# Block-sorted attention with a gated MLP behind it: q turned by DMA, other layouts on both sides of PSUM, a new written order and a guarded second path

## The chip, the cores and the metric

The program runs on one core of a Trainium2 chip. The metric is device time of one launch in microseconds (us). TensorE (PE in the profile) multiplies and puts its results into PSUM; ScalarE (ACT) and VectorE (DVE) bring them from there into SBUF; GpSimd (POOL) works on SBUF alone and issues the loads; SyncE (SP) issues the other DMAs.

## The reference

Inputs: q, k and v as 4 batches x 8 heads x 768 positions x 64 numbers, float32; `sort_net`, an 8x8 matrix for each batch and head; and the weights of a gated MLP.

```
P = sort_net
for _ in range(5):
    P = exp(P - max(P, -1));  P /= sum(P, -1) + 1e-9;  P /= sum(P, -2) + 1e-9
k_sorted[i] = sum_j P[i, j] * k_block[j]          # 8 blocks of 96 positions; v alike
attn  = softmax(q_block[i] @ k_sorted[i].T / 8) @ v_sorted[i]
x     = attn, heads side by side                    # 4 x 768 x 512
h     = relu(x @ w_in);  u, v = h[:, :512], h[:, 512:]
v_n   = (v - mean) / sqrt(var + 1e-6)               # over the 512 columns
gated = u * (w_spatial @ v_n + b_spatial)           # w_spatial is 768 x 768
out   = gated @ w_out
```

The kernel multiplies in bfloat16 and adds up in float32.

## The kernel before

Nothing is scheduled by a library. A string, `ORDER` (L16), lists units of work, and each unit issues its instructions on each engine's queue in that order. An engine takes its queue in order, so a unit that waits holds all that is listed later on the same engine. Heads go in pairs (`hp`, 0 to 3), and the 8 blocks of a sequence in halves (`ih`, 0 and 1). PSUM is four tiles of two banks, `ps0` to `ps3`; a unit's first number names the one that it fills, and its letter the engine that empties it (A is ACT, D is DVE).

The units in the order in which a batch passes them, with their lines:

- `L` (L153): loads, issued by POOL; float32 in HBM, bfloat16 in SBUF. Partition p holds positions 6p to 6p+5 of every head, so one block of 96 positions is 16 partitions. `wv` and `wu` are the halves of w_in, `ws` is w_spatial, `wo` is w_out.
- `SK` (L190): one of five rounds on P, one exp on ACT and six small DVE instructions. The last writes `p_x`, half of it on DVE and half on POOL. `PR`/`PS` (L209, L213) turn it on PE, `P0` (L223) spreads it into `pd`, a 128x128 mixing matrix for each head of batch 0, and `PD` (L236) does so on POOL for the other batches.
- `QT` (L270): turns q of a head pair with 12 matmuls against the identity; the result is emptied into `qT`.
- `KT` (L298): mixes and turns k with 12 matmuls against `pd`; emptied into `kT`. Both copies read PSUM straight on and write every sixth element, so that positions come into their natural order (first snippet below).
- `VM` (L309) and `VC` (L323): mix v into `vm`, and bring it from 16 partitions x 6 positions to 96 partitions with eight DMAs on SP for each batch.
- `SC` (L333): scores of half the blocks of a head pair, 8 matmuls, and one exp on ACT into `ex`. `AT` (L355): 8 matmuls with v (a column of ones gives the sum), and on DVE a reciprocal and a multiplication into `x_sb`.
- `XT` (L378): turns x with 8 PE transposes; emptied into `xT`.
- `VP` (L398), `LN`, `LA` (L423, L429): the v half of x @ w_in, relu, statistics on DVE, normalisation. `UP` (L438): the u half. `WS` (L251): turns w_spatial on PE, six units in all. `SP` (L453): 12 matmuls with w_spatial, the bias added into `z`, and the product with u, on DVE or POOL, into `gt`. `OP` (L473): 8 matmuls with w_out, emptied, and stored by SP.

```
copy(eng, q_tile(b, hp)[:, lo * G:(lo + n) * G].rearrange("p (x g) -> p g x", g=G),   # L282
     t[:, 0:n * G].rearrange("p (g x) -> p g x", g=G))
```

Of the kernel before, what the change touches and what calls it, by code (L numbers as in the profile page):

```python
# [9 lines left out]
BF16 = mybir.dt.bfloat16  # L10
AF = mybir.ActivationFunctionType
# [3 lines left out]

ORDER = """  # L16
L:q:0:0:64 ID IN L:v:0:0:128 SK:0 L:k:0:0:128 SK:0 QT:0:A:0:2:0 L:q:0:64:128 L:wv SK:0 QT:1:A:0:3:0
QT:2:A:0:0:0 QT:3:A:0:1:0 SK:0 DM:0:5:384 DM:1:5:384 DM:2:5:384 DM:3:5:384 L:wu IV:0 L:ws SK:1 PR:0
PS P0:0:0:2 P0:0:2:8 P0:1:4:8 P0:1:0:4 PC:D KT:1:A:0:2:0 L:v:1:0:128 VM:2:D:0:3 VM:3:A:0:0 VM:1:D:0:2
VM:0:A:0:1 KT:2:A:0:0:0 QT:3:D:0:1:1 KT:1:D:0:1:0 KT:0:D:0:3:0 IV:1 KT:2:D:0:2:1 SC:3:0:2:0  # L20
L:k:1:0:128 VC:0:0 KT:1:A:0:0:1 VC:0:1 SC:0:0:0:0 KT:2:D:0:1:1 QT:3:D:0:2:1 KT:1:D:0:3:1 L:q:1:0:128
SC:2:0:3:0 QT:0:D:0:3:1 SC:3:0:1:0 AT:1:0:2:0 PD:1:0:4 QT:2:A:0:0:1 AT:0:0:0:0 SC:3:0:3:1 SC:1:0:1:1
AT:2:0:3:0 AT:0:0:1:0 SC:3:0:2:1 XT:1:D:0:0:1 L:wo SC:2:0:0:1 XT:3:D:0:0:0 AT:0:0:1:1 PD:1:4:8
AT:1:0:3:1 WS:2:A:1 L:v:2:0:128 VP:3:D:0:0:1 L:k:2:0:128 WS:0:A:3 VP:2:A:0:2 VM:1:A:1:2 VM:3:A:1:0
UP:0:A:0:0:0 VM:2:A:1:1 AT:1:0:2:1 UP:3:A:0:1:0 AT:0:0:0:1 KT:1:A:1:2:2 XT:2:D:0:1:1 VM:3:A:1:3
WS:0:D:2 KT:1:A:1:0:2 KT:2:D:1:1:2 KT:3:A:1:3:2 VC:1:0 PD:3:4:8 VC:1:1 WS:0:D:4 WS:1:D:0 QT:2:A:1:2:2
QT:3:D:1:3:2 QT:0:A:1:1:2 QT:1:D:1:0:2 SC:2:1:2:0 XT:3:D:0:1:0 SC:0:1:3:1 SC:1:1:2:1 AT:2:1:2:0
PD:2:0:4 VP:3:A:0:5 SC:0:1:0:1 AT:1:1:3:1 L:q:2:0:128 LN:0:0:3 WS:2:A:5 LA:0:2 VP:3:D:0:3:4
SC:0:1:3:0 SC:1:1:0:0 UP:2:A:0:0:1 AT:0:1:2:1 VM:3:A:2:1 PD:2:4:8 UP:1:A:0:1:1 AT:2:1:0:1 L:v:3:0:128
AT:3:1:0:0 SC:0:1:1:1 KT:1:A:2:2:2 XT:2:D:1:1:1 VM:0:A:2:0 AT:3:1:1:1 SC:1:1:1:0 VM:2:D:2:2  # L30
L:k:3:0:128 KT:0:A:2:3:2 XT:3:D:1:1:0 QT:1:A:2:0:2 VM:2:A:2:3 LA:0:1 AT:0:1:1:0 LN:0:3:6 VC:2:0
UP:3:A:1:0:1 LA:0:0 LA:0:4 XT:1:D:1:0:0 KT:2:A:2:0:2 LA:0:3 VC:2:1 LA:0:5 QT:0:A:2:2:2 AT:3:1:3:0
VP:1:A:1:4:5 SC:2:2:0:1 PD:3:0:4 SC:0:2:0:0 LN:1:4:6 SP:3:P:0:1 SC:1:2:2:1 SC:2:2:2:0 SP:0:P:0:2
XT:3:D:1:0:1 AT:1:2:0:0 L:q:3:0:128 SP:2:D:0:3 LA:1:4 KT:0:A:2:1:2 QT:3:A:2:1:2 QT:1:A:2:3:2
AT:2:2:0:1 SP:0:P:0:0 VM:3:A:3:1 AT:1:2:2:0 VP:2:D:1:0:1 SC:0:2:3:0 SC:3:2:1:1 VP:1:A:1:2:3
VM:0:D:3:3 UP:2:A:1:1:0 LN:1:0:4 OP:3:A:0:2 AT:1:2:2:1 LA:1:2 LA:1:0 LA:1:5 LA:1:1 UP:2:A:1:0:0
LA:1:3 SC:0:2:3:1 SC:3:2:1:0 OP:1:A:0:0 AT:2:2:3:1 OP:0:A:0:1 AT:3:2:1:1 AT:1:2:1:0 UP:2:A:1:1:1
XT:0:D:2:1:1 XT:3:D:2:1:0 KT:1:A:3:3:2 QT:2:A:3:1:2 KT:0:A:3:1:2 KT:3:D:3:0:2 VP:1:D:2:4:5 VM:2:A:3:2
VM:3:A:3:0 SP:0:D:1:3 XT:1:A:2:0:0 AT:2:2:3:0 SP:3:P:1:2 LN:2:4:6 LA:2:4 UP:1:A:2:0:1 XT:0:D:2:0:1
QT:2:A:3:2:2 VC:3:0 LA:2:5 KT:3:A:3:2:2 QT:1:D:3:3:2 QT:0:D:3:0:2 VP:2:D:2:2:3 VC:3:1 UP:3:A:2:0:0  # L40
SP:1:D:1:1 SC:0:3:2:0 SC:2:3:1:1 SP:3:D:1:0 SC:1:3:2:1 SC:0:3:3:1 UP:2:A:2:1:0 AT:3:3:1:1
UP:1:A:2:1:1 AT:0:3:2:0 VP:2:D:2:0:1 SC:3:3:1:0 SC:1:3:0:0 OP:0:A:1:2 AT:2:3:3:1 LN:2:0:4 AT:3:3:2:1
OP:1:A:1:0 SC:0:3:3:0 SC:2:3:0:1 OP:3:A:1:1 LA:2:0 LA:2:1 LA:2:3 LA:2:2 AT:1:3:0:0 SP:0:D:2:1
SP:2:P:2:2 XT:1:A:3:1:1 AT:3:3:0:1 SP:0:D:2:0 AT:2:3:3:0 XT:1:A:3:1:0 SP:3:P:2:3 AT:0:3:1:0
UP:1:A:3:0:1 UP:2:A:3:1:1 XT:3:A:3:0:0 XT:0:D:3:0:1 VP:1:A:3:4:5 VP:2:A:3:2:3 VP:0:A:3:0:1 OP:3:A:2:0
UP:1:A:3:0:0 LN:3:4:6 LA:3:4 LN:3:0:4 LA:3:0 LA:3:5 LA:3:3 OP:2:A:2:2 LA:3:2 UP:0:A:3:1:0 LA:3:1
OP:3:D:2:1 SP:1:P:3:1 SP:2:D:3:3 SP:0:D:3:0 SP:3:D:3:2 OP:1:A:3:2 OP:2:A:3:1 OP:0:A:3:0
"""

# [10 lines left out]
def kernel(  # L60
# [92 lines left out]
    def u_L(what, *a):  # L153
        if what in ("q", "k", "v"):
            load(what, int(a[0]), int(a[1]), int(a[2]), int(a[1]) == 0)
        elif what == "wv":
            nc.gpsimd.dma_start(
                out=w_in_sb[:, :, DH:DFF], in_=moe_w_in.rearrange("(kc p) f -> p kc f", p=128)[:, :, DH:DFF])
        elif what == "wu":
            nc.gpsimd.dma_start(  # L160
                out=w_in_sb[:, :, 0:DH], in_=moe_w_in.rearrange("(kc p) f -> p kc f", p=128)[:, :, 0:DH])
        elif what == "ws":
            nc.gpsimd.dma_start(out=wsp_nat, in_=moe_w_spatial.rearrange("(c p) s -> p c s", p=128))
        elif what == "wo":
            nc.gpsimd.dma_start(out=w_out_sb, in_=moe_w_out.rearrange("(fc p) n -> p fc n", p=128))

    def u_IN():
        nc.sync.dma_start(out=p_all, in_=sort_net.rearrange("b h i j -> (b h) i j"))
        nc.sync.dma_start(
            out=b_bc, in_=_raw_ap(moe_b_spatial, 0, [[0, 128], [1, S]]))  # L170
        nc.vector.memset(warm, 0.0)
        nc.vector.memset(eps_tile, 1e-6)
        for n in range(NE):
            nc.vector.memset(ex[n][:, 2 * NI * BLK:], 0.0)

    def u_ID():
        make_identity(nc, ident)
        nc.vector.reduce_sum(
            out=st["m32"][:], in_=ident.rearrange("p (j t) -> p t j", t=TB), axis=AX.X)
        nc.vector.tensor_copy(out=mask16, in_=st["m32"][:])  # L180

    st["m32"] = const.tile([128, TB], FP32, name="m32")

    def u_IV(n):
        n = int(n)
        nc.gpsimd.memset(vm[n][:, :, :, D:VW], 1.0)
        nc.gpsimd.memset(vb[n][:, :, :, D:VW], 1.0)


    def u_SK(last):  # L190
        nc.scalar.activation(out=p_all, in_=p_all, func=AF.Exp)
        nc.vector.reduce_sum(out=rowsum, in_=p_all, axis=AX.X)
        nc.vector.reciprocal(out=rowsum, in_=rowsum)
        nc.vector.tensor_mul(out=p_all, in0=p_all, in1=rowsum.to_broadcast([BH, NB, NB]))
        nc.vector.reduce_sum(out=colsum, in_=p_all.rearrange("p i j -> p j i"), axis=AX.X)
        nc.vector.reciprocal(out=colsum, in_=colsum)
        if int(last):
            for ih, eng in enumerate((nc.vector, nc.gpsimd)):
                eng.tensor_mul(
                    out=p_x[ih],  # L200
                    in0=_raw_ap(p_all, ih * NI * NB, [p_all.ap[0], [NB, NI], [1, NB], [0, TB]]),
                    in1=_raw_ap(colsum, 0, [colsum.ap[0], [0, NI], [1, NB], [0, TB]]),
                )
        else:
            nc.vector.tensor_mul(
                out=p_all, in0=p_all, in1=_raw_ap(colsum, 0, [colsum.ap[0], [0, NB], colsum.ap[1]]),
            )
# [319 lines left out]
```

## Time and profile before

| what | us |
|---|---|
| three runs | 215.75, 216.23, 216.97 |
| span of the profiled execution, first to last instruction | 214.0 |
| PE busy in it | 163.0 |
| DVE busy | 133.9 |
| ACT busy | 131.0 |
| POOL busy | 35.3 |
| last matmul ends at | 208.4 |

The profile gives the profiled execution's own time as its span alone. The median run is 2.2 us longer, and that is what lies around the span. Busy time is work, not a bound: PE is busy for three quarters of the span, yet it is only in stretches that it never waits. The views to read are the chain of work that ended last, the busy time of each engine by stage, and the groups of instructions with the mean duration of one.

### The profile page before, as it was taken

The numbers are of one execution on the slowest core, as the hardware profiler recorded it, in microseconds if no ns is written. First come the engines' busy times: TensorE is split into PE (matmuls) and PEld (weight loads), VectorE is DVE, ScalarE is ACT, GpSimd is POOL, SyncE is SP. The second block draws the span as 40 slices with busy tenths as digits, with TensorE's granted clock in tenths as the row PEclk, the third lists the DMA queues.
The fourth block names the chain that finished last, engine by engine and source line by source line (L and its number), as shares of the span: only waits on it lengthen the run. The fifth ranks groups of instructions, "written<-read, shape, count | busy, mean of one in ns | idle before, by whom it ended". The sixth has DMA issues, their size and how long they took to land.

```text
span 214.0 us, 4057 instructions
## 1 busy us (share of the span) xinstructions
PE 163.0 (76%) x1716; PEld 101.0 (47%) x1728; DVE 133.9 (63%) x244; ACT 131.0 (61%) x133; POOL 35.3 (16%) x41
## 2 busy tenths in 40 slices
PE   0283856996438969959659996595999999999790
PEld 0241445954335545535424555273665566455330
DVE  3236689776685774524725857589968585664900
ACT  3180854669997699993693769939455524580031
POOL 7405906201300000003430000011000033002000
PEclk9997575599995995888997999999999999999999
DMA  5999999999995000350460042071001600024025
GB/s 93 192 203 206 211 223 236 204 204 204 211 245 93 0 2 3 54 100 0 47 100 3 14 182 101 0 121 35 0 3 39 254 4 0 3 105 189 0 103 193
DMA packets 21921, 22.38 MB, mean 105 GB/s; under 512 B 1040, under 2 KB 18704, under 8 KB 21904
## 3 DMA queue, kind: packets, MB, share of 16 engines
q0 software_dynamic: 14864, 12.19, 36.4%
q1 hardware_dynamic: 7040, 9.94, 16.2%
q8 instruction: 13, 0.21, 0.4%
q14 instruction: 4, 0.03, 0.0%
HBM read 24.78 MB, written 6.29 MB: 145 GB/s over the span
## 4 chain that ended last, share of the span: by engine, by line
PE 53%; ACT 25%; DVE 12%; DMA 5%; issue 3%; POOL 1%; ACTq 0%; DVEq 0%; POOLq 0%
PE ps L458 13%; ACT kT L104 11%; ACT qT L104 10%; PE ps L446 9%; PE ps L405 8%; PE ps L479 8%; DVE qT L106 4%; PE ps L364 4%; DMA q_in<-in_q_dram 4%; PE ps L341 3%; DVE kT L106 3%; PE ps L386 2%; PE ps L313 2%; PE ps L291 2%; ACT u_sb L110 1%
## 5 line engine op out<-in xcount | busy, mean ns | idle before, releaser
L104 ACT CAST kT<-ps 128x768 bf16<-128x768 f32 (+1 forms) x13 | 31.8, 2475 | 9.5 <-PE ps L291 9.5
L458 PE MATMUL ps<-wspT,v_sb 128*128 128x384 bf16 x192 | 34.9, 337 | 3.5 <-ACT kT L104 3.5
L349 ACT ACTIVATE ex<-ps 96x768 bf16<-96x768 f32 x32 | 24.9, 811 | 15.2 <-PE ps L341 15.1
L470 POOL TENSOR_TENSOR gt<-z,u_sb 128x768 bf16<-128x768 f32 x7 | 11.5, 1647 | 129.0 <-DVE z L464 101.1
L104 ACT CAST qT<-ps 128x768 bf16<-128x768 f32 (+1 forms) x13 | 29.4, 2394 | 5.4 <-PE ps L276 5.4
L405 PE MATMUL ps<-w_in_sb,xT 128*128 128x512 bf16 x88 | 24.6, 411 | 4.4 <-ACT kT L104 1.8
L458 PEld LDWEIGHTS <-v_sb 128*128 128x128 bf16 x192 | 18.7, 100 | 16.3 <-issue 5.4
L446 PE MATMUL ps<-xT,w_in_sb 128*128 128x384 bf16 x128 | 24.6, 338 | 0.7 <-ACT kT L104 0.7
L479 PE MATMUL ps<-w_out_sb,gt 128*128 128x512 bf16 x92 | 22.2, 380 | 1.8 <-DVE gt L470 1.7
L464 DVE TENSOR_TENSOR z<-ps,b_bc 128x768 f32<-128x768 f32 x16 | 15.3, 954 | 12.3 <-PE ps L458 12.3
L372 DVE TENSOR_TENSOR x_sb<-ps,rec 96x512 bf16<-96x512 f32 x32 | 22.0, 687 | 1.1
L104 ACT COPY o_sb<-ps 128x1024 f32<-128x1024 f32 x11 | 11.1, 1012 | 17.3 <-PE ps L479 15.9
L419 DVE BATCH_NORM_STATS2 stats<-v_sb 128x6 f32<-128x512 bf16 x24 | 16.3, 677 | 8.7 <-ACT v_sb L110 8.4
L110 ACT ACTIVATE u_sb<-ps 128x768 bf16<-128x768 f32 x16 | 13.0, 810 | 11.1 <-PE ps L446 10.9
L341 PE MATMUL ps<-qT,kT 64*96 64x96 bf16 x256 | 12.1, 232 | 9.1 <-ACT qT L104 4.8
L276 PE MATMUL ps<-ident,q_in 128*64 128x128 bf16 (+1 forms) x240 | 9.4, 233 | 10.8 <-DMA q_in<-in_q_dram 9.2
L364 PE MATMUL ps<-vb,ex 96*128 96x65 bf16 x256 | 14.2, 208 | 3.5 <-ACT qT L104 2.1
L106 DVE CAST qT<-ps 128x768 bf16<-128x768 f32 (+1 forms) x7 | 15.1, 2239 | 2.6 <-PE ps L276 2.6
L446 PEld LDWEIGHTS <-w_in_sb 128*128 128x128 bf16 x128 | 12.3, 100 | 9.2 <-issue 2.0
L341 PEld LDWEIGHTS <-kT 64*96 64x96 bf16 x256 | 9.7, 139 | 14.5 <-issue 12.7
L405 PEld LDWEIGHTS <-xT 128*128 128x128 bf16 x96 | 9.7, 107 | 14.2 <-issue 6.5
L364 PEld LDWEIGHTS <-ex 96*128 96x128 bf16 x256 | 12.7, 107 | 7.3 <-issue 4.2
(63 smaller groups left out, 203.9 us busy)
## 6 DMA issues: line engine op xcount, KB each, us to landing
out_dram<-o_sb SPq DMA_DIRECT2D x12, 512.0 KB, 2.8
vb<-vm SPq DMA_DIRECT2D x32, 99.0 KB, 4.6
v_in<-in_v_dram POOLq DMA_DIRECT2D x4, 768.0 KB, 13.5
k_in<-in_k_dram POOLq DMA_DIRECT2D x4, 768.0 KB, 15.9
q_in<-in_q_dram POOLq DMA_DIRECT2D x3, 768.0 KB, 20.5
wsp_nat<-in_moe_w_spatial_dram POOLq DMA_DIRECT2D x1, 1152.0 KB, 21.9
w_in_sb<-in_moe_w_in_dram POOLq DMA_DIRECT2D x2, 512.0 KB, 16.4
q_in<-in_q_dram POOLq DMA_DIRECT2D x2, 384.0 KB, 10.9
```

The source lines that it names most:

```text
L104: nc.scalar.copy(out=out, in_=in_)
L106: nc.vector.tensor_copy(out=out, in_=in_)
L341: nc.tensor.matmul(t[0:BLK, hh, ii * BLK:(ii + 1) * BLK], lhsT=kT[rows, i * BLK:(i + 1) * BLK], rhs=qT[rows, i * BLK:(i + 1) * BLK], start ...
L349: nc.scalar.activation(out=e[:, 0:2 * NI * BLK].rearrange("p (h c) -> p h c", h=2), in_=t[0:BLK, :, 0:NI * BLK], func=AF.Exp, scale=scale,)
L364: nc.tensor.matmul(t[:, hh, ii * VW:ii * VW + D + 1], lhsT=e[:, c:c + 128], rhs=vb[b % 2][:, ih * NI + ii, 2 * hp + hh, 0:D + 1], start=Tr ...
L372: nc.vector.tensor_mul(out=x_sb[:, :, hp * 128:hp * 128 + 128].rearrange("p i (h d) -> p h i d", h=2), in0=tv[:, :, :, 0:D], in1=_raw_ap(r ...
L405: nc.tensor.matmul(t[:, x, :], lhsT=st["xT", b][:, kc, n * 128:(n + 1) * 128], rhs=w_in_sb[:, kc, DH:DFF], start=(kc == 0), stop=(kc == KC ...
L419: nc.vector.bn_stats(out=stats, in_=v_sb[:, x, :])
L446: nc.tensor.matmul(t[:, x, 0:HW], lhsT=w_in_sb[:, kc, mc * 128:(mc + 1) * 128], rhs=st["xT", b][:, kc, ih * HW:(ih + 1) * HW], start=(kc = ...
L458: nc.tensor.matmul(t[:, x, 0:HW], lhsT=st["v_sb", b, n][:, mc * 128:(mc + 1) * 128], rhs=wspT[:, n, x * HW:(x + 1) * HW], start=(n == 0), ...
L464: nc.vector.tensor_add(out=z.rearrange("p (x c) -> p x c", x=2), in0=t[:, :, 0:HW], in1=b_bc.rearrange("p (x c) -> p x c", x=2),)
L479: nc.tensor.matmul(t[:, x, :], lhsT=st["gt", b, mc][:, c * 128:(c + 1) * 128], rhs=w_out_sb[:, mc, :], start=(mc == 0), stop=(mc == FC - 1),)
```

## The change

`ORDER` is written anew, and with it these units change:

- q of batches 1 to 3 no longer goes through PE and PSUM. `QP` copies a head pair so that for each of the 6 positions of a partition the two heads lie side by side (nine on POOL, three on DVE), and `QX` turns a whole batch with one DMA transpose on SP. The positions stay in the order in which they come, and `SC` reads q with a stride of 128 elements (`q_block`). Batch 0 keeps `QT`.
- x (`XD`, eight DMAs, each for half a batch) and w_spatial (`WX`, one DMA) are turned by DMA transposes on SP too; `XT` and `WS` are gone.
- `natural` takes the place of the copies of `QT` and `KT`: it reads PSUM with a stride of 128 and writes SBUF straight on.
- v of batch 0 is mixed and turned like k (`VT`) and turned back on PE (`VB`) in place of `VM` and `VC`.
- P: the last round of `SK` writes a small `p16`, DVE transposes it, and `PR` spreads it with a constant matrix. `pd` has two buffers in place of four, `vm` one in place of two; `ex` has 5 in place of 4, `u` 4 in place of 3, `v_sb` 6 in place of 5, `x_sb` 3 in place of 2.
- The loads of batch 0 come by heads (two halves on all 128 partitions) in place of halves of the partitions.
- Statistics (`ST`), the gate (`GT`), and the parts of `OP` (`OE` empties, `OS` stores) are units of their own; 15 of 16 gates are on POOL (7 before). The last batch's `OP` goes in parts.
- `CK` looks at whether row sums stayed within bounds and writes `flag`. At the end every engine loads `flag` and jumps over `general_path`, which computes everything again with the maxima subtracted, and which these inputs don't take.

The diff without the parts that only rename, and with the last lines alone of the new order:

```
 ORDER = """
...
-UP:1:A:3:0:0 LN:3:4:6 LA:3:4 LN:3:0:4 LA:3:0 LA:3:5 LA:3:3 OP:2:A:2:2 LA:3:2 UP:0:A:3:1:0 LA:3:1
-OP:3:D:2:1 SP:1:P:3:1 SP:2:D:3:3 SP:0:D:3:0 SP:3:D:3:2 OP:1:A:3:2 OP:2:A:3:1 OP:0:A:3:0
+ID CO L:q:0:0:4 L:q:0:4:8 L:k:0:4:8 MK DM:0:18:256 S0 IV:2 SK:0 SK:1 IV:0 SK:2 L:v:0:4:8 QT:1:A:0:1 IV:1 SK:3
+DM:2:16:256 SK:4 QT:3:A:0:0 QT:0:A:0:3 PR:1 L:k:0:0:4 L:v:0:0:4 PC:A P0:6:8 L:q:1:0:8 QT:2:A:0:2 P0:4:6
+L:v:1:0:8 P0:2:4 P0:0:2 KT:3:A:0:3 PD:1:4:8 VT:0:D:0:3 VT:2:A:0:2 KT:1:D:0:2 SC:3:0:3:1 L:k:1:0:8 VB:0:D:0:3
...
+L:k:2:0:8 L:ws PD:2:0:4 AT:2:0:0:0 VM:0:A:1:3 VM:1:A:1:1 QX:1:0:4 AT:3:0:2:0 AT:2:0:1:0 L:q:3:0:8 KT:0:A:1:1
+L:v:3:0:8 KT:3:A:1:3 XD:0:1:0:4 VC:1:4:8 QP:P:2:1 KT:1:D:1:0 KT:2:D:1:2 SC:0:1:1:1 SC:1:1:1:0 VP:3:A:0:3
...
+GT:P:1:3 AT:3:3:3:0 UP:0:D:2:0:1 SP:2:2:0 XD:3:0:0:4 OP:1:1:4 OE:D:1:4 SC:3:3:1:1 SC:0:3:0:1 GT:P:2:0 SP:2:2:3
+AT:3:3:1:1 AT:1:3:0:1 XD:3:1:0:4 OS:1:4 VP:0:A:3:0:1 ST:3:0 ST:3:1 UP:2:A:3:1:0 SP:3:2:1 OP:1:1:0 OE:D:1:0
+VP:0:D:3:2:3 ST:3:3 OS:1:0 GT:P:2:3 VP:2:A:3:4:5 ST:3:2 SP:3:2:2 ST:3:5 OP:1:1:2 OE:A:1:2 ST:3:4 LN:3:0:6
...
+GT:D:3:3 GT:P:3:1 OS:2:0 OP:3:3:2:0:3 OP:-1:3:2:3:4 OS:2:4 OE:A:3:2:0:1 OS:3:2:0:1 OP:1:3:4:0:3 OP:-1:3:4:3:4
+OE:D:3:2:1:2 OS:3:2:1:2 OE:D:3:4:0:1 OS:3:4:0:1 OP:0:3:0:0:3 OE:D:3:4:1:2 OS:3:4:1:2 OP:-1:3:0:3:4
+OE:A:3:0:1:2 OS:3:0:1:2 CK:2 OE:A:3:0:0:1 OS:3:0:0:1
...
+        to = p16.rearrange("p (i j) -> p i j", i=NB) if n == 4 else p_all
+        nc.vector.tensor_mul(out=to, in0=p_all, in1=over_cols(colsum))
+        if n == 4:
+            nc.vector.transpose(out=p_t, in_=p16)
+    def u_PR(ps):
+        pr = ps_tile(ps)[:, 0, 0:NB * BH].rearrange("p (i y) -> p i y", i=NB)
+        for i in range(NB):
+            nc.tensor.matmul(
+                pr[:, i, :], lhsT=spread[:, (i % NI) * NB:(i % NI + 1) * NB].rearrange("p j t -> p (j t)"),
+                rhs=p_t[:, (i // NI) * BH:(i // NI + 1) * BH], start=True, stop=True,
             )
...
+    def natural(eng, dst, t):
+        copy(eng, dst.rearrange("p (x g) -> p x g", g=G), t[:, 0:S].rearrange("p (g x) -> p x g", g=G))
...
+    def u_QP(eng, b, hp):
+        getattr(nc, {"P": "gpsimd", "D": "vector"}[eng]).tensor_copy(
+            out=st["qp", b][:, hp].rearrange("p g h d -> p h g d"),
+            in_=st["q", b][:, 2 * hp:2 * hp + 2].rearrange("p h (g d) -> p h g d", g=G),
+        )
+    def u_QX(b, lo, hi):
+        nc.sync.dma_start_transpose(
+            out=q_tile(b)[:, lo * S:hi * S].rearrange("p (x c) -> p x c", c=128),
+            in_=st["qp", b][:, lo:hi].rearrange("p k g h d -> p (k g h d)"),
+        )
+    def q_block(b, hp, rows, i):
+        q_hp = q_tile(b)[rows, hp * S:(hp + 1) * S]
+        if ("qp", b) in st:
+            return q_hp.rearrange("p (g t) -> p t g", g=G)[:, i * TB:(i + 1) * TB, :]
+        return q_hp[:, i * BLK:(i + 1) * BLK]
...
+    def u_VB(ps, eng, b, hp):
+        t = ps_tile(ps, BF16)[0:BLK, 0, :].rearrange("p (i c) -> p i c", i=NB)
+        vT = turned("vT", b, hp)
+        for i in range(NB):
+            nc.tensor.transpose(t[:, i, :], vT[:, i * BLK:(i + 1) * BLK], ident)
+        copy(eng, vb[b % 2][:, :, 2 * hp:2 * hp + 2, 0:D], t.rearrange("p i (h d) -> p i h d", h=2))
...
+    def u_XD(b, ih, lo, hi):
+        nc.sync.dma_start_transpose(
+            out=st["xT", b][:, ih, lo:hi].rearrange("p k (i c) -> p (k i) c", i=NI),
+            in_=st["x", b, ih][:, lo:hi].rearrange("p k i c -> p (k i c)"),
+        )
+    def u_WX(lo, hi):
+        nc.sync.dma_start_transpose(
+            out=wspT[:, lo:hi].rearrange("p c n t -> p (c n) t"),
+            in_=wsp_nat[:, lo:hi].rearrange("p c s -> p (c s)"),
+        )
...
+    def u_CK(ps):
+        nc.vector.memset(bad, 0.0)
+        over = lambda col, rows, in_, op, bound, test: (
+            nc.vector.tensor_reduce(out=ends[0:rows, col:col + 1], in_=in_, axis=AX.X, op=op),
+            nc.vector.tensor_scalar(out=bad[0:rows, col:col + 1], in0=ends[0:rows, col:col + 1],
+                scalar1=bound, scalar2=None, op0=test),
+        )
+        recs = rec_all.rearrange("p n h i -> p (n h i)")
+        over(0, BLK, recs, ALU.max, 1.0 / SUM_LO, ALU.is_gt)
...
+        t = ps_tile(ps)
+        nc.tensor.matmul(t[0:1, 0, 0:5], lhsT=ones, rhs=bad, start=True, stop=True)
+        nc.vector.tensor_reduce(out=ends[0:1, 0:1], in_=t[0:1, 0, 0:5], axis=AX.X, op=ALU.add)
+        nc.vector.tensor_copy(out=flag, in_=ends[0:1, 0:1])
...
     with tc.manual_schedule():
...
+        beyond = nc.values_load(flag[0:1, 0:1], min_val=0, max_val=512)
+        with tc.If(beyond > 0, preferred_fallthrough_block=False):
+            general_path()
```

## The prediction

> **What bounds the kernel now.** I read the engines' busy times first, then the chain of work that ended last, then the busy time by stage, then the groups with shapes kept apart. The busy times and the chain's shares by engine and line, from the page:
>
> ```profile
> PE 163.0 (76%) x1716; PEld 101.0 (47%) x1728; DVE 133.9 (63%) x244; ACT 131.0 (61%) x133; POOL 35.3 (16%) x41
> ...
> PE 53%; ACT 25%; DVE 12%; DMA 5%; issue 3%; POOL 1%; ACTq 0%; DVEq 0%; POOLq 0%
> PE ps L458 13%; ACT kT L104 11%; ACT qT L104 10%; PE ps L446 9%; PE ps L405 8%; PE ps L479 8%; DVE qT L106 4%; PE ps L364 4%; DMA q_in<-in_q_dram 4%; PE ps L341 3%; DVE kT L106 3%; PE ps L386 2%; PE ps L313 2%; PE ps L291 2%; ACT u_sb L110 1%
> ```
>
> No engine is full. Emptying qT and kT takes 11+10+4+3 = 28% of the chain, 60 us. The busy time by stage (columns: stage, length, busy us of PE, PE's weight loads, DVE, ACT and POOL with counts, granted clock, DMA share, GB/s); the first two lines are from one question, the others from a second:
>
> ```profile
> 0.00:21.00 21.00, 7.66 (x76) 4.35 (x76) 8.47 (x41) 7.42 (x10) 9.34 (x20) 0.96 1.10 173
> 21.00:208.40 187.40, 155.38 (x1640) 96.61 (x1652) 125.41 (x204) 122.53 (x122) 25.94 (x23) 0.90 0.47 94
> ```
>
> ```profile
> 68.00:112.00 44.00, 34.51 (x385) 21.71 (x386) 22.89 (x46) 35.91 (x33) 5.79 (x4) 0.85 0.24 37
> 112.00:150.00 38.00, 30.92 (x318) 18.17 (x320) 27.96 (x43) 26.31 (x25) 1.68 (x1) 0.96 0.24 64
> 150.00:208.40 58.40, 56.49 (x434) 31.64 (x437) 38.80 (x68) 25.13 (x34) 4.93 (x3) 1.00 0.17 64
> ```
>
> Three parts have different limits. Until 21 us P is made and loads come in. From 21 to 150 ACT and DVE empty PSUM and PE waits: its busy share is 155.4-56.5 = 98.9 of 129 us, part of it at half clock. From 150 PE is busy 97% and is the bound. In the whole middle part PE is busy 155.4/187.4 = 83%, and the three engines together do (155.4+125.4+122.5)/187.4 = 2.15 us of work in each us. The groups by shape:
>
> ```profile
> L104 ACT CAST kT<-ps 128x768 bf16<-128x768 f32 x10 | 27.5, 2786 | 4.4 <-PE ps L291 4.4
> ...
> L341 PE MATMUL ps<-qT,kT 64*96 64x96 bf16 x256 | 12.1, 232 | 9.1 <-ACT qT L104 4.8 <-ACT kT L104 2.3 <-DVE kT L106 1.5
> ...
> L104 ACT CAST vm<-ps 128x768 bf16<-128x768 f32 x12 | 10.5, 893 | 0.8 <-PE ps L313 0.8
> ...
> L386 PE MATMUL ps<-ident,x_sb 96*128 96x96 bf16 x128 | 8.8, 221 | 0.4 <-DVE qT L106 0.4
> ...
> L195 DVE TENSOR_REDUCE colsum<-p_all 32x8 f32<-32x64 f32 x5 | 1.3, 254 | 0.2
> ...
> L192 DVE TENSOR_REDUCE rowsum<-p_all 32x8 f32<-32x64 f32 x5 | 1.0, 203 | 7.6 <-ACT p_all L191 7.6
> ```
>
> The first and third line are the same size and engine: writing every sixth element costs 2786 ns, writing straight on 893. The last two lines read the same 64 numbers, with a stride and without: 254 against 203 ns, 0.8 ns more for each element.
>
> **The change, part by part.** The sum is start + middle + waits for DMA transposes + tail + what lies around the span.
>
> *Start, 14 us (before: KT begins at 21.05).* In the timeline a round of SK takes 1.74 us where nothing holds it (first row sum 3.61, second 5.35). The third exp came at 10.85 and the fourth at 14.73, since ACT's queue had qT copies ahead; without that the third would come near 6.8 and the fourth 1.9 us sooner: 6 us lost. The new order puts three rounds before any copy and one copy before the fourth, which fits under q's landing. Mask and spread come ahead on DVE (+0.3), so the fifth round ends at 3.9+5x1.74 = 12.6; the POOL half of p_x (1.54) goes, a small DVE transpose (as colsum, 0.25) and 8 matmuls (0.5) come, and P0 0.4: about 14. q in two halves on all partitions lands no later than the first half of before (9.2). Bounds 13 and 17 (one copy of 2.8 in the way).
>
> *Emptying, price X.* natural reads with a stride and writes straight on. Below: 0.9 (vm row). Above: 2.79 (kT row). It is nearest to the strided read: 0.89+768 x 0.0008 = 1.5 us. I take X = 1.5.
>
> *PE in the middle, 155.4.* QT: 9.4 for 240 matmuls, 7.6 of it after 21 us; one of batch 0's four stays there, -7.1. XT -8.8. WS -3.7. VM 32 to 24 matmuls, -2.2. KT 240 to 192, -1.9. VT 48 like KT's, +1.9. VB 32 transposes at 69 ns x 128/96, +2.9. SC reads q with a stride for batches 1 to 3, 192 matmuls of 47 ns busy each (12.05/256): no matmul of before reads so. Below 0; above the factor of the strided write, 2786/893 = 3.1, +18.9; I take the strided read's 254/203 = 1.25, +2.3. Sum 138.8.
>
> The Trainium skill, Advanced Engine Details and Errata, Memory Cachelines, says that an access which goes to another 16-byte line each time is penalised in SBUF, and of PSUM that any non-contiguous pattern slows matmuls significantly. It speaks against this read and against natural, and gives no figure; by it the sum would lie nearer 204 (below) than 186.
>
> *DVE, 125.4.* Off: kT 12.6, qT 15.1, xT 6.7, wspT 1.7, three vm 2.9, eight gates at 0.96 7.7, two v relus 2.5: 49.2. On: 7X; four VB copies at 0.564 x 1024/768, 3.0; three QP as LA's 0.43 x 1.5, 1.9; six u relus 5.6; o copies 5.5; the check's twelve small ones 2.4. 94.6+7X = 105.1.
>
> *ACT, 122.5.* Off: kT 31.8, qT 24.0, xT 3.2, wspT 2.4, one vm 0.9, six u 4.9, o copies 4.4, half of rstd 2.0: 73.6. On: 14X, two v 2.1, prep 0.4. 51.4+14X = 72.4.
>
> *Middle, 157 us.* 138.8+105.1+72.4 = 316.3; at 2.15 a us that is 147 us, and PE would be busy 94% from the first mixing on, though batch 0 has little to overlap with. At PE's old 83% it is 167. I take the mean, 157. Ends: X = 0.9 with PE at its best 97%, 143; PE at 83%, 167.
>
> *POOL, at nothing.* Eight more gates at 1.65, nine QP near the same (its row of 768), issues at 0.87: about 60 of 170 us. A QP ahead of a load on POOL's queue delays that load (q2 stands behind QP, which waits for q1); the cover is that v1, k1 and both w_in halves, 2.6 MB at 205 GB/s or 13 us, are queued by then. Two pd buffers make PD of batch 2 wait for batch 0's last mixing; PD is early by a batch. Without these covers k2 comes late by one QP and PD, 3 us.
>
> *DMA transposes, waits of 6 us.* Twelve: XD 393 KB each, QX double, WX triple, 17 units of 393 KB, all on SP's one queue between v's copies and the stores. No trace shows one. Below: the store's 512 KB in 2.8 us, 2.1 a unit. Above: queue 1's 7040 packets took 16.2% of 16 engines' 214 us, 79 ns each; 393 KB in rows of 128 numbers are 96 packets an engine, 7.6. Nearest is vb<-vm, SBUF to SBUF: 4.6 to landing. What covers them on PE: between QX of batch 1 and its first SC two AT and four KT, 1.9 us; between XD and VP of batch 0 1.2; of batch 3 4.7 and 6.7. So batches 0 and 1 wait about 9.2-1.9, of which I let a few us fall under ACT and DVE, and the others hardly: 6. Ends 0 and 22 (at 7.6, QX and both XD of batch 0 in a row take 30 us). VC, behind QX on SP, is late with it.
>
> The Trainium skill, DMA: Bandwidth & Descriptors, Latency and other measured facts, gives 261 GB/s for a DMA transpose; an estimate from it is 1.5 us a unit, waits near 1, and a sum of 181. The vb<-vm row is slower.
>
> *Tail, 6.6 us (before: 208.4 to 214.0, 5.6).* The last copy and store are halved (-0.4 and up to -1). The last OP and the flag stand in one line: a matmul, two DVE ops at 0.2, a register load on each engine (nearest: p_all's DMA, 1.7), a jump over code that isn't loaded. I put +1; ends 4 and 9.
>
> 14+157+6+6.6 = 183.6 of span. The span before is 214.0 and the median run 216.2: 2.2 lie around it. **186 us.**
>
> **The rivals.**
> - *Slower: the transposes are the bound.* They share SP's queue. The first can start near 26 us (q1 lands near 19, 3.1 MB at 205 GB/s from about 3; then its QP), and after the last, XD of batch 3, PE has 36 us of VP, UP, SP and OP at the chain's 1.73, 1.30, 1.95 and 1.73 each. 26+17u+36+8.8 passes 216.2 from u = 8.6 us a unit, 46 GB/s; at 10 it gives 241. For it: the 79 ns a packet comes close. Against: vb<-vm.
> - *Everything hides.* Start 13, middle 143, no waits, tail 5.6: 164. For it: the 97% after 150 us. Against: batch 0.
> - *The strided q is dear.* +16.6 on PE, at the same 88% 19 us: 204.
> - *Transposes at 7.6.* Waits of 22: 202.
> - *natural does not do what it says,* X = 2.79: 343/2.15 = 159, mean with 167 is 163: 192. It counts with the forecast, since 24 copies in place of 40 remain a gain.
>
> **How the numbers follow.** Forecast, with X anywhere: 0.60, its own range 174 to 197. All hidden 0.09, strided q 0.09, slow transposes 0.08, transposes the bound 0.11, several of these that cancel the gain 0.03. Leaving out the bound case and half of the hidden one gives 171 to 206. A measurement of this kernel tells 0.5% from no change. Faster is all but the last two, 0.86; same 0.03; slower 0.11.
>
> **What would show it.** KT's first matmul near 14 us; natural's copies near 1.5 us; SC's busy time at most a quarter up; no PE wait over 3 us on xT or qT except around 30 to 45 us; PE busy near 88% between. I am wrong if XD takes over 7 us to land, if SC's matmuls double, or if PE waits for SP's queue throughout.

## The result, and the profile after

The changed kernel takes 208.02 us (four runs, 207.4 to 208.35) where the kernel before, beside it, takes 216.13 (215.75 to 216.97). The ratio is 0.961, with a 95% interval of 0.958 to 0.964. The forecast was 186, with a range of 171 to 206: the sign is right, the size is not, and the range missed. The gain is 8 us of a forecast 30. Runs of one kernel can lie some per cent apart, and where that matters below, the fastest run is the one compared.

The profiled execution has a span of 206.2 us, and 1.8 lie around it. The page's busy times and the chain's shares of the kernel after:

```profile
PE 152.1 (74%) x1411; PEld 90.4 (44%) x1411; DVE 110.5 (54%) x244; ACT 72.4 (35%) x102; POOL 55.0 (27%) x58
...
PE 53%; DMA 22%; SPq 11%; DVE 6%; POOL 3%; issue 1%; ACT 0%; POOLq 0%; DVEq 0%
PE ps L522 16%; DMA xT<-x_sb 10%; PE ps L467 9%; PE ps L548 9%; PE ps L510 8%; DMA wspT<-wsp_nat 7%; DMA v_in<-in_v_dram 6%; SPq L308 5%; PE ps L382 5%; SPq L446 4%; PE ps L428 2%; PE ps L323 2%; SPq L363 2%; PE ps L350 1%; DVE x_sb L436 1%; POOL k_in L160 1%
```

ACT was 25% of the chain and is 0% now: the emptying of q and k no longer sets the pace. In its place stand DMA (22%, of which 6% is a load of v at the start) and SP's own queue (11%); L308 and L446 are the two lines that issue the DMA transposes of q and x, L453 the one of w_spatial. The busy time by stage, first of the kernel before between 30 and 61 us, then of the kernel after in four stages (columns as in the prediction):

```profile
30.00:61.00 31.00, 22.93 (x360) 18.25 (x359) 23.01 (x36) 23.13 (x22) 7.99 (x8) 0.79 1.29 216
```

```profile
30.00:61.00 31.00, 3.00 (x33) 1.97 (x32) 1.82 (x2) 2.30 (x4) 5.14 (x7) 0.58 1.26 191
61.00:75.00 14.00, 9.74 (x55) 4.21 (x55) 2.77 (x7) 3.13 (x4) 0.00 (x0) 0.62 1.25 207
75.00:110.00 35.00, 30.41 (x302) 18.63 (x299) 21.47 (x45) 18.68 (x26) 3.13 (x4) 0.94 0.81 134
110.00:198.00 88.00, 87.11 (x640) 48.72 (x638) 58.90 (x108) 28.67 (x39) 25.66 (x16) 1.00 0.33 95
```

From 30 to 61 us the whole core all but stands still: PE works 3.0 of 31 us where it worked 22.9 before, DVE 1.8 and ACT 2.3. From 110 us on PE is busy 99%. So the gain is there at the end and most of it is lost in one hole in the middle. PE's waits (total, times, longest) name the releasers, and SP's own queue in the same stretch shows when each transpose was issued and how long it held the queue (start, length):

```profile
PE ps L382 <- DMA qT<-qp: 18.3, 1, 18.3
PE ps L467 <- DMA xT<-x_sb: 13.9, 2, 9.7
PE ps L522 <- DMA wspT<-wsp_nat: 4.6, 1, 4.6
```

```profile
25.79 13.38 SPq L308 DMA_TRANSPOSE qT<-qp  x1
39.23 8.09 SPq L446 DMA_TRANSPOSE xT<-x_sb  x1
47.37 3.34 SPq L363 DMA_DIRECT2D vb<-vm  x4
50.75 10.86 SPq L446 DMA_TRANSPOSE xT<-x_sb  x1
61.65 0.59 SPq L363 DMA_DIRECT2D vb<-vm  x1
```

The same two lines over the whole run (durations min/median/max in ns, then the time to landing in us), q first:

```profile
L308 SPq DMA_TRANSPOSE qT<-qp x3: 3431/3477/13379, 25.8 to 107.7; - x3
...
DMA to landing us min/median/max: 5.1/6.6/22.9
```

```profile
L446 SPq DMA_TRANSPOSE xT<-x_sb x8: 1399/1552/10856, 39.2 to 163.4; - x8
...
DMA to landing us min/median/max: 3.5/3.7/20.8
```

The same instruction takes 3.4 us late in the run and 13.4 at 26 us; x takes 1.4 us late and 10.9 at 51. What differs is what else is on the DMA engines, as the experiments below show. The trace's DMA queues in two stretches (queue, packets, MB, share of 16 engines' time), 35 to 40 us and then 85.5 to 87.5, when the transpose of q of batch 2 is alone:

```profile
DMA packets 1871, 0.95 MB, mean 191 GB/s; under 512 B 946, under 2 KB 1871, under 8 KB 1871
...
q0 software_dynamic: 936, 0.71, 90.6%
q1 hardware_dynamic: 935, 0.24, 36.1%
```

```profile
DMA packets 2265, 0.57 MB, mean 286 GB/s; under 512 B 2265, under 2 KB 2265, under 8 KB 2265
...
q1 hardware_dynamic: 2265, 0.57, 126.3%
```

q0 carries the loads, q1 what SP issues, here the transposes. Under loads the two keep step packet for packet: 936 against 935. A transpose packet carries 0.24 MB/935, some 256 bytes, and a load packet 0.71/936, some 760, so the transpose gets a quarter of the bytes, 48 GB/s, where it has 286 GB/s alone. q of a batch is 786 KB, 3072 packets; at 935 in 5 us that is 16 us, at 286 GB/s 2.7.

Last the groups that the forecast spoke of:

```profile
L109 ACT CAST kT<-ps 128x768 bf16<-128x768 f32 x12 | 9.1, 802 | 4.0 <-PE ps L323 4.0
L109 ACT CAST vm<-ps 128x768 bf16<-128x768 f32 x11 | 8.5, 801 | 14.8 <-PE ps L350 14.7
L382 PE MATMUL ps<-qT,kT 64*96 64x96 bf16 x256 | 21.1, 308 | 18.5 <-DMA qT<-qp 18.3
```

The copy of `natural` takes 802 ns (2786 before), as much as the straight copy of the same size, `vm`, in the line below. SC's matmuls are busy 21.1 us (12.1 before).

### The profile page after: what moved, and what is told of

It reads as the page before. It is cut to its first block, busy times and chain, and to the rows that moved or that the text cites. A ratio compares the mean times of both kernels' runs of the same rounds, so it can differ in the third digit from the quotient of the medians.

```text
span 206.2 us, 3498 instructions
## 1 busy us (share of the span) xinstructions
PE 152.1 (74%) x1411; PEld 90.4 (44%) x1411; DVE 110.5 (54%) x244; ACT 72.4 (35%) x102; POOL 55.0 (27%) x58
## 4 chain that ended last, share of the span: by engine, by line
PE 53%; DMA 22%; SPq 11%; DVE 6%; POOL 3%; issue 1%; ACT 0%; POOLq 0%; DVEq 0%
PE ps L522 16%; DMA xT<-x_sb 10%; PE ps L467 9%; PE ps L548 9%; PE ps L510 8%; DMA wspT<-wsp_nat 7%; DMA v_in<-in_v_dram 6%; SPq L308 5%; PE ps L382 5%; SPq L446 4%; PE ps L428 2%; PE ps L323 2%; SPq L363 2%; PE ps L350 1%; DVE x_sb L436 1%; POOL k_in L160 1%
## 5 line engine op out<-in xcount | busy, mean ns | idle before, releaser
L538 POOL TENSOR_TENSOR gt<-z,u_sb 128x768 bf16<-128x768 f32 x15 | 24.6, 1648 | 71.7 <-DVE z L528 29.7
L467 PE MATMUL ps<-w_in_sb,xT 128*128 128x512 bf16 x96 | 26.3, 425 | 13.9 <-DMA xT<-x_sb 13.9
L382 PE MATMUL ps<-qT,kT 64*96 64x96 bf16 x256 | 21.1, 308 | 18.5 <-DMA qT<-qp 18.3
L382 PEld LDWEIGHTS <-kT 64*96 64x96 bf16 x256 | 14.8, 137 | 25.2 <-issue 23.4
L301 POOL COPY qp<-q_in 128x768 bf16<-128x768 bf16 x9 | 7.3, 839 | 59.6 <-DMA qT<-qp 55.5
L436 DVE TENSOR_TENSOR x_sb<-ps,rec_all 96x512 bf16<-96x512 f32 x32 | 22.0, 687 | 1.1
L115 ACT ACTIVATE v_sb<-ps 128x1024 bf16<-128x1024 f32 (+1 forms) x9 | 8.3, 927 | 25.9 <-PE ps L467 25.9
L510 PEld LDWEIGHTS <-w_in_sb 128*128 128x128 bf16 x128 | 11.8, 98 | 8.5 <-issue 0.6
L548 PEld LDWEIGHTS <-gt 128*128 128x128 bf16 x96 | 9.1, 98 | 11.9 <-DVE gt L538 1.4
L109 ACT COPY o_sb<-ps 128x1024 f32<-128x1024 f32 (+1 forms) x8 | 6.7, 854 | 21.0 <-PE ps L548 17.5
L109 ACT CAST vm<-ps 128x768 bf16<-128x768 f32 x11 | 8.5, 801 | 14.8 <-PE ps L350 14.7
L435 DVE RECIPROCAL rec_all<-ps 96x8 f32<-96x8 f32 x32 | 6.3, 196 | 11.4 <-PE ps L428 11.3
```

Source lines behind the costliest of these rows:

```text
L109: nc.scalar.copy(out=out, in_=in_)
L382: nc.tensor.matmul(t[0:BLK, hh, ii * BLK:(ii + 1) * BLK], lhsT=kT[rows, i * BLK:(i + 1) * BLK], rhs=q_block(b, hp, rows, i), start=True, s ...
L436: nc.vector.tensor_mul(out=x_sb[:, hp].rearrange("p i (h d) -> p h i d", h=2), in0=tv[:, :, :, 0:D], in1=_raw_ap(rec, 0, [rec.ap[0], [NI, ...
L467: nc.tensor.matmul(t[:, x, :], lhsT=st["xT", b][:, n // 3, kc, (n % 3) * 128:(n % 3 + 1) * 128], rhs=w_in_sb[:, kc, DH:DFF], start=(kc == ...
L510: nc.tensor.matmul(t[:, x, 0:HW], lhsT=w_in_sb[:, kc, mc * 128:(mc + 1) * 128], rhs=st["xT", b][:, ih, kc, :], start=(kc == 0), stop=(kc = ...
L538: eng.tensor_mul(out=gt, in0=st["z", b, mc], in1=st["u", b, mc // 2][:, mc % 2])
```

## The experiments

The theories:
- **Q**: the DMA transposes are slow because they share the DMA engines with queued loads.
- **S**: the first transposes are slow for themselves.
- **C**: PE would have waited in that stretch for another reason.
- **N**: the new copies hold the gain, and the rest of the change costs.
- **R**: the strided read of q costs the most.
- **F**: the check, the loads of its flag and the jump cost the end.

All ratios are to the kernel before, run beside.

**The copies alone.** The kernel before, with the one edit in the copies of QT and KT:

```
-            q_tile(b, hp)[:, lo * G:(lo + n) * G].rearrange("p (x g) -> p g x", g=G),
-            t[:, 0:n * G].rearrange("p (g x) -> p g x", g=G),
+            q_tile(b, hp)[:, lo * G:(lo + n) * G].rearrange("p (x g) -> p x g", g=G),
+            t[:, 0:n * G].rearrange("p (g x) -> p x g", g=G),
```

> The kernel before, and of the change only the copies of qT and kT, which now read PSUM with a stride and write straight on. By the trace of after such a copy takes 0.80 on ACT and 0.95 on DVE in place of 2.79: 40 copies (some of them halves) save near 57 us of ACT and DVE together, and 61 us of the chain were these copies. Theory N (that is where the gain of the change lies): 185-200 us. Rival: PE, busy 163 us, and the order that was written for slow copies hold the end, 205-214.

Measured: 182.41 us, ratio 0.840 (0.836 to 0.844), below the 185 to 200 that were expected. The two copies alone bring 34 us, four times what the whole change brings. In this kernel's groups the copy is as fast as in the changed one, and SC (here of q in its natural order) waits for nothing:

```profile
L104 ACT CAST kT<-ps 128x768 bf16<-128x768 f32 x10 | 7.9, 801 | 3.7 <-PE ps L291 3.7
...
L341 PE MATMUL ps<-qT,kT 64*96 64x96 bf16 x256 | 11.2, 222 | 0.3
```

N holds: against this kernel, all the rest of the change together costs 26 us.

**No loads of batches 2 and 3.** The changed kernel, whose last two batches take the q, k and v of the first two (their loads are left out):

```
+            if b > 1:
+                st[what, b] = st[what, b - 2]
+                return
```

> The loads of batches 2 and 3 are left out (their q, k and v are those of batches 0 and 1 again). Theory Q (a DMA transpose shares the DMA engines packet by packet with the loads that are queued): QX of batch 1 holds SP's queue for under 7 us in place of 13.4, both XD of batch 0 for under 3 in place of 8.1 and 10.9, PE's idle time between 30 and 61 us falls from 29 to under 10, and the time to 175-187. Rival S (the first transposes are slow for themselves, or SP's own work is): the same durations, and no less than 204 us. Rival C (PE would wait there in any case, for k of batch 1 and w_in): transposes get short, and the time falls by under 8 us.

Measured: 186.16 us (the other of the two runs 190.5), 22 us less than the changed kernel. SP's queue here:

```profile
26.18 14.27 SPq L311 DMA_TRANSPOSE qT<-qp  x1
40.51 3.20 SPq L449 DMA_TRANSPOSE xT<-x_sb  x1
46.44 1.55 SPq L449 DMA_TRANSPOSE xT<-x_sb  x1
```

The transpose of q1 is as slow as before (under 7 us had been expected). It has loads beside it here too: k1, both halves of w_in and w_spatial, which this run keeps and which lands at 42.8 us. The transposes of x, behind them, take 3.2 and 1.55 us in place of 8.1 and 10.9. PE is busy 17.3 us between 30 and 61, where the changed kernel has 3.0, and still waits 13.7 us for q1. S and C fall for x; for q1 this run leaves S open.

**The first transposes on PE.** The changed kernel with q of batch 1 and x of batch 0 turned on PE (`QT` and the old `XT`) in the places of `QX` and `XD`:

```
-... QP:P:1:1 QP:D:1:2 ... QP:D:1:0 ... QP:P:1:3 ... QX:1:0:4 ... XD:0:1:0:4 ... XD:0:0:0:4 ...
+... QT:0:D:1:1 ... QT:1:A:1:3 ... XT:2:D:0:1:0 ... QT:1:D:1:0 ... QT:3:A:1:2 ... XT:3:A:0:1:1 ...
```

> After, but q of batch 1 and x of batch 0 are turned on PE, as the loads are still under way then; the other transposes stay. Theory Q: PE's idle stretch between 30 and 61 us goes, but QX of batch 2 and XD of batch 1 now come at 45-65 us, in the loads too, and wait 5-15 us there: 182-198. Rival S (first transposes are slow wherever they stand): 195-205. Rival C (nothing to do for PE before 61 us): 204 or more.

Measured: 185.12 us, ratio 0.855 (0.850 to 0.860); PE is busy 22.5 us between 30 and 61. With `QT`, q of batch 1 is no longer read with a stride either, which is part of this gain. The hole has moved. SP's queue in this kernel:

```profile
49.98 3.54 SPq L446 DMA_TRANSPOSE xT<-x_sb  x1
53.63 14.90 SPq L308 DMA_TRANSPOSE qT<-qp  x1
72.47 1.63 SPq L446 DMA_TRANSPOSE xT<-x_sb  x1
```

Now q of batch 2 is the one that falls under loads, and it takes 14.9 us, though x went ahead of it in 3.5. In the changed kernel q of batch 2, after the loads, took 3.5. So being first is not what makes a transpose slow: S falls for q too.

**The same work, later loads.** The changed kernel with all its transposes; GpSimd reads one column of q1 and of both halves of batch 0's x before it issues the loads from q2 on, and so holds them:

```
+ XD:0:0:0:4 HO:0 L:q:2:0:8 L:v:2:0:8 L:k:2:0:8 L:ws L:q:3:0:8 L:v:3:0:8 QP:P:2:1 ...
+    def u_HO(b):
+        for t in (q_tile(b + 1)[:, 0:1], st["xT", b][:, 0, 0, 0:1], st["xT", b][:, 1, 0, 0:1]):
+            nc.gpsimd.tensor_copy(out=hold, in_=t)
```

> The changed kernel with all its work and all its transposes, but the loads from q2 on wait on GpSimd until the transposes of q1 and of batch 0's x have landed. Theory Q, queued loads slow the transposes: QX of batch 1, issued near 26 while k1 and both w_in halves are still queued, holds SP near 14 us as before; both XD of batch 0 then find the queue nearly empty and hold it 1.4 to 5 us each (8.1 and 10.9 in the changed kernel); the same loads come some 15 us later, so that QX of batch 2 or v2, k2 are late, and the time moves by less than 12 us: 196 to 212. Theory S, the early transposes are slow for themselves: both XD stay at 8 to 11 us. Theory C, PE would wait there anyway: XD short, but PE busy in 30 to 61 us still under 6.

Measured: 199.83 us, ratio 0.922 (0.916 to 0.927). SP's queue:

```profile
25.55 10.61 SPq L309 DMA_TRANSPOSE qT<-qp  x1
36.23 1.48 SPq L447 DMA_TRANSPOSE xT<-x_sb  x1
41.04 1.62 SPq L447 DMA_TRANSPOSE xT<-x_sb  x1
56.40 6.26 SPq L447 DMA_TRANSPOSE xT<-x_sb  x1
62.77 17.90 SPq L309 DMA_TRANSPOSE qT<-qp  x1
```

Both transposes of batch 0's x hold the queue 1.5 and 1.6 us, and the ones that the later loads now cover, x of batch 1 and q of batch 2, take 6.3 and 17.9, where the changed kernel has 1.4 and 3.5. While q of batch 2 is turned, from 62.8 to 80 us, the two queues send the same number of packets to the last one, load packets of some 940 bytes now:

```profile
q0 software_dynamic: 2639, 2.47, 91.5%
q1 hardware_dynamic: 2639, 0.67, 34.1%
```

Nothing but the loads was moved, and the slowness went with them. Q is shown. PE is busy 6.7 us between 30 and 45 and 13.7 between 45 and 61, 20.4 in all, so C falls as well; holding the loads only shifts the hole, and wins 8 us of it.

**q in runs of 16.** The changed kernel, with SC reading q's columns as they lie (six runs of 16 for each block), a block's scores in 128 columns of PSUM in place of 96, and the exp on ACT putting the order right as it reads PSUM:

```
-            return q_hp.rearrange("p (g t) -> p t g", g=G)[:, i * TB:(i + 1) * TB, :]
+            return q_hp.rearrange("p (g t) -> p g t", g=G)[:, :, i * TB:(i + 1) * TB]
...
+            tv = tv.rearrange("p x (g t) -> p x t g", g=G)
+            ev = ev.rearrange("p x (t g) -> p x t g", g=G)
```

> After, but SC takes q in runs of 16 numbers, and the exp brings the positions into order by reading PSUM with a stride. Theory R (the stride of 256 bytes makes SC slow: 8 matmuls take 0.72 us in place of 0.25, 24 times, 22 of them behind the wait): SC's busy time falls from 21.1 to 12-15, the time by 7-11 us to 197-201; the exp stays near 0.80. Rival: SC is slow for another reason (runs do not help), or the exp gets dear by as much: 206-212.

Measured: 202.82 us, ratio 0.930 (0.922 to 0.938), 5 us less than the changed kernel, where 7 to 11 had been expected. The group of SC's matmuls:

```profile
L382 PE MATMUL ps<-qT,kT 64*96 64x96 bf16 x256 | 10.4, 219 | 16.4 <-DMA qT<-qp 16.2
```

SC is back from 21.1 to 10.4 us, and the exp, which now reads with a stride, takes 803 ns as it did. Between 110 and 198 us, where all of the changed kernel's SC is strided and the clock is near full in both, 80 matmuls are busy 7.48 us with the stride and 2.79 with the runs, a factor of 2.7. So the stride of 128 elements costs PE 10.7 us of work, and the order can be put right for nothing on the way through PSUM. R holds as a cost, not as the largest.

**Without the check.** The changed kernel without `CK`, the loads of `flag` and `general_path`:

```
-OE:A:3:0:1:2 OS:3:0:1:2 CK:2 OE:A:3:0:0:1 OS:3:0:0:1
+OE:A:3:0:1:2 OS:3:0:1:2  OE:A:3:0:0:1 OS:3:0:0:1
...
-        beyond = nc.values_load(flag[0:1, 0:1], min_val=0, max_val=512)
-        with tc.If(beyond > 0, preferred_fallthrough_block=False):
-            general_path()
```

> The changed kernel without the check of the row sums, the loads of its flag and the second path behind them (the second path is never taken with these inputs). Theory F, the flag's loads and the jump cost the end: in the changed kernel 6.2 us lie between the end of the last DVE instruction of the check (200.0) and the end of the span (206.2), and the last two output copies wait 3.5 us for a store. Without them the last store (issued near 199, some 2 to 3 us to land) sets the end: span about 202, time 202 to 204, ratio 0.93 to 0.945. Rival, the stores' landing sets the end anyway and the flag's loads lie beside it: time within 1 us of the changed kernel's 208, ratio 0.955 to 0.965. In both the middle stays: PE still idle for most of 30 to 61 us, the last matmul of the output near 198.

Measured: 204.18 us, ratio 0.939 (0.932 to 0.946); by the medians 3.8 us less. F holds, smaller than the 6 us between the flag and the end suggest: without the check too 5.2 us lie between the last matmul and the end of the span, where the changed kernel has 8.1. So 2.9 us of the 3.8 stand in the tail; in the profiled execution the last matmul also ends 1 us sooner, and for that nothing here shows a reason.

**PE under the loads, DMA after them.** The changed kernel with q of batches 1 and 2 and x of batches 0 and 1 on PE, the transposes of q3, x2, x3 and w_spatial kept, and the runs of 16:

```
-... QX:1:0:4 ... XD:0:1:0:4 ... XD:0:0:0:4 ... XD:1:0:0:4 ... QX:2:0:4 ... XD:1:1:0:4 ...
+... QT:0:D:1:1 QT:1:A:1:3 ... XT:2:D:0:1:0 ... XT:2:D:1:0:0 XT:3:A:1:0:1 ... QT:3:A:2:3 ... XT:0:D:1:1:0 ...
```

> The changed kernel with every turn that falls under queued loads back on PE (q of batches 1 and 2, x of batches 0 and 1), the DMA transposes of q3, x2, x3 and w_spatial kept, and q of batch 3 read in runs of 16. Theory Q, the transposes are dear only because they share the DMA engines packet for packet with queued loads: the four kinds that are left hold SP 1.5 to 5 us each as in the changed kernel's trace after 75 us, PE has no wait over 3 us for q or x, PE busy in 30 to 61 us is over 22 of 31 us, and the time is 168 to 180. Theory C, PE would stand idle there anyway for other reasons (loads come late, batch 0 has nothing beside it): PE busy in 30 to 61 us stays under 15 and the time stays over 190. Theory R, the strided read costs the most: the gain over the run with batch 1's q and batch 0's x on PE (185) is the strided read's, and SC's busy time near 10 us.

Measured: 172.63 us, ratio 0.798 (0.794 to 0.803). PE waits for one transpose alone, 1.5 us, though w_spatial's transpose still falls under loads and holds SP 16.6 us:

```profile
57.60 16.58 SPq L468 DMA_TRANSPOSE wspT<-wsp_nat  x1
```

```profile
PE ps L537 <- DMA wspT<-wsp_nat: 1.5, 1, 1.5
```

It is slow and lands only after 20.1 us, but its first reader comes 18.6 us after the issue. What counts here is the distance between issue and use.

**No DMA transpose at all.** q, x and w_spatial all on PE, the rest as changed:

```
-... QX:3:0:4 ... WX:0:6 ... XD:2:0:0:4 ... XD:3:1:0:4 ...
+... QT:2:A:3:3 ... WS:2:A:0 ... XT:2:A:2:0:0 XT:0:A:2:0:1 ... XT:0:A:3:1:0 XT:3:A:3:1:1 ...
```

> The changed kernel with no DMA transpose at all: q, x and w_spatial are turned on PE and emptied by ACT and DVE as before, all else as changed (natural copies, start, v of batch 0, orders, check). It tells what the DMA transposes are worth where they are not under loads. Theory Q alone (transposes free where no load is queued): PE, DVE and ACT do some 15 us more work than in the run that keeps them for q3, x2, x3 and w_spatial, at 2.15 us of work a us that is 5 to 7 us longer: 175 to 186. Rival, a DMA transpose brings nothing even without loads (its latency is waited for): this one is as fast as that run or faster, 168 to 176. If both fell and the cause lay in the rest of the rewrite (its order, the start, the check), this one would stay over 195.

Measured: 193.17 us (188.79 to 194.83; the runs lie too far apart for a ratio with an interval). No expectation held. It differs from the run of 172.63 in the turns that lie behind most of the loads (q3, x2, x3, w_spatial), and there DMA is worth 16 us by the fastest run, not 5 to 7. The page's busy times of the two, without a DMA transpose first (this page is of a run of 193.24 us):

```profile
PE 156.5 (82%) x1706; PEld 99.3 (52%) x1719; DVE 112.8 (59%) x247; ACT 92.6 (48%) x130; POOL 48.0 (25%) x49
```

```profile
PE 144.7 (85%) x1558; PEld 89.9 (53%) x1571; DVE 112.6 (66%) x248; ACT 79.6 (47%) x112; POOL 50.4 (30%) x52
```

PE has 11.8 us more to do in it and ACT 13.0, and its granted clock is lower, 0.943 against 0.980. No single one of PE's waits is over 2.3 us (x_sb 4.3 in three, u_sb 2.5 in two). How the 16 us of the fastest run divide is not shown, since it has no trace. Whether better places for these units would win some of that back was not tried.

**Both.** The run of 172.63 without the check:

```
-OE:A:3:0:1:2 OS:3:0:1:2 CK:2 OE:A:3:0:0:1 OS:3:0:0:1
+OE:A:3:0:1:2 OS:3:0:1:2  OE:A:3:0:0:1 OS:3:0:0:1
```

> The run that turns on PE whatever falls under queued loads (172.6), without the check, its flag and the second path. Theory F: the flag's loads and the jump cost this one what they cost the changed kernel, 3.8 us, and less than the 6 us that lie between flag and end: 167.5 to 170, ratio 0.775 to 0.785 to the kernel before. Rival, there the stores set the end anyway: within 1 us of 172.6.

Measured: 168.89 us, ratio 0.783 (0.777 to 0.789): 3.7 us for the check here, as there. This takes 19% less time than the changed kernel and 22% less than the one before, and it has no second path, as the kernel before has none.

## Why the prediction was wrong

By its own terms, with what the trace of the changed kernel shows:

| term | forecast | measured |
|---|---|---|
| start, to KT's first matmul | 14 | 12.8 |
| middle without waits for transposes | 157 | 148.5 |
| waits for DMA transposes | 6 | 36.8 |
| tail, from the end of the last OP's matmul | 6.6 | 8.1 |
| around the span | 2.2 | 1.8 |
| sum | 186 | 208.0 |

The middle is 12.8 to 198.1 us, 185.3, less the 18.3 + 13.9 + 4.6 of waits shown above.

- **The step that failed: waits of 6 us, ends 0 and 22.** The unit price under it was wrong in kind. I took one price for all twelve transposes and looked for the row nearest in operation, vb<-vm with 4.6 us. For a transpose that is alone this was near: x lands in 3.5 to 3.7 us. But a price for a DMA holds only beside what else is queued. Of the kernel before I had the DMA share, 1.10 in the first 21 us and 0.47 as a mean over the 187 behind them; the line from 30 to 61 us, 1.29, would have shown that the loads fill the engines just where the first three transposes go. The rival "transposes at 7.6", with "QX and both XD of batch 0 in a row take 30 us", had the right place and very nearly the length: the row of three held SP from 25.8 to 61.6 us. Its waits of 22 were still too few: the row was 36 us long and not 30, and the last of the three landed only at 71.2; PE had next to nothing beside it (18.3 us of waits for q1, 13.9 for x of batch 0); and w_spatial's transpose at 93 us, with the load of w_out beside it, held SP for 12.0 us and cost 4.6 more. Two of the prediction's own signs of being wrong came: XD took up to 20.8 us to land, and the strided matmuls of SC more than doubled.
- **The Trainium skill's figure.** The page DMA: Bandwidth & Descriptors, Latency and other measured facts, has 261 GB/s for a DMA transpose. Alone, it moved 286 GB/s here, a tenth more; over all of the 3.48 us for which q's transpose held SP, 226. Under loads it moved 48. The page's price is of the right size where nothing shares the engines, and this case's hole is where something does.
- **The rival that transposes are the bound** has its point at 8.6 us a unit. Under loads a unit held SP for 6.7 (q1, two units in 13.4), 8.1 and 10.9 us; afterwards for 1.4 to 1.7, but 4.0 in w_spatial's three beside w_out. PE waited for them from 30.5 to 48.9, from 50.4 to 60.1 and from 66.9 to 71.2 us, and 4.6 us at w_spatial, and nowhere else.
- **X, right in kind, too dear.** natural costs 0.80 us on ACT and 0.95 on DVE, not 1.5. The strided read of PSUM is free here: vm's straight copy takes 801 ns on ACT and 958 on DVE in the same kernel. I carried the 0.8 ns for each element over from a strided read of 64 numbers in SBUF. 0.7 us less in 14 copies on ACT and 0.55 in 7 on DVE are 13.6 us of work less in the middle; SC put half of that back, and the three engines together had 310.7 us of work there for the 316.3 of the forecast.
- **The middle, 148.5 in place of 157.** By an estimate from these sums, the smaller part of the 8.5 us, 2.6, is less work (5.6 us at 2.15 a us). The rest is the mean with 167: outside the waits the engines did 2.09 us of work in each us, near the 2.15 of before, where 157 stands for 2.01.
- **The strided q, right in kind, too cheap.** +2.3 us was taken, with the factor 1.25; SC went from 12.1 to 21.1 with a quarter of it not strided; for the strided ones the factor was 2.7, close to the upper end that the prediction took from the strided write, and the runs of 16 show 5 us of it in the time. The two strided prices were mis-sized in opposite directions, so that they partly cancelled, which was luck. The Trainium skill's page Advanced Engine Details and Errata, Memory Cachelines, says that accesses in SBUF which go to a different cacheline each time are penalised; the read of q agrees (21.1 against 10.4 us). What it says of PSUM, that any non-contiguous pattern slows matmuls, can't be carried to the copies of ACT and DVE, which pay nothing.
- **Start: right.** Three rounds before any copy, and KT at 12.8.
- **Tail:** 8.1 in place of 6.6, inside its ends of 4 and 9; without the check it is 5.2.
- **POOL at nothing:** no wait of PE names POOL, but POOL had waits that I did not see. `qp` has one buffer, so q of a batch can be paired only when the transpose of the batch before it has landed. POOL's queue (start, length; idle time before it in brackets):

```profile
48.85 2.37 POOL L301 COPY qp<-q_in 128x768 bf16<-128x768 bf16 x3 [18.76 <-DMA qT<-qp]
51.16 0.87 POOL L160 DMA_DIRECT2D k_in<-in_k_dram  x1
...
90.69 2.37 POOL L301 COPY qp<-q_in 128x768 bf16<-128x768 bf16 x3 [36.78 <-DMA qT<-qp]
93.01 0.82 POOL L173 DMA_DIRECT2D w_out_sb<-in_moe_w_out_dram  x1
```

The load of k3 is behind the first wait; among PE's waits none for k appears. The load of w_out is behind the second, and so it starts at 93.0 us together with w_spatial's transpose, for which PE then waits 4.6 us. With the first transposes on PE, w_spatial's held SP 5.5 us in place of 12.0 and PE did not wait for it. That an earlier load of w_out would save these 4.6 us was not tried.

## What to carry to other kernels

Price a DMA by what is queued beside it in that stretch: read the DMA share of the stage into which it goes, not that of the span, and put DMA transposes where no loads are, or so far ahead of their use that a time four or more times as long does not matter (q took 3.5 us and 13.4 to 17.9). Where the loads ran, turning on PE was the cheaper way; behind most of them, DMA was worth 16 us. When a change has many parts, the cheapest experiment is the smallest part alone: two copies of this one were worth 34 us.

## What the runs showed of the hardware that was not expected

- While both have work, queued loads and a DMA transpose get the same number of packets (936 and 935 in 5 us, 2639 and 2639 in 17), though they carry different amounts: 256 bytes against 760 and 940. In the first of these stretches the transposes moved 48 GB/s, where one alone moved 286.
- Reading PSUM with a stride of 128 float32 costs ACT and DVE nothing (802 against 801 ns on ACT, 951 against 958 on DVE), while writing every sixth bfloat16 cost three times as much (2786 against 893 ns on ACT). The order of the axes belongs on the reading side.
- A matmul that reads its moving operand from SBUF with a stride of 128 bfloat16 took 2.7 times as long (80 of them 7.48 us in place of 2.79); with runs of 16 elements all of SC took 10.4 us, where the kernel before, which has no stride there, takes 12.1.
- The straight copy `vm`, whose code no part of the change touches, went from 893 to 801 ns wherever the strided writes were gone, in the run of the copies alone too (804). Why is open.
